# Loading v: two adjacent heads' columns written as one dimension

## The chip, the cores and the metric

The kernel runs on one core of a Trainium2 chip. A core has five engines with their own instruction streams, run in order: PE (matrix multiplication), DVE, ACT and POOL (elementwise work), and SP, which here only issues transfers. Transfers between the chip's main memory and the core's on-chip memory run on 16 DMA engines. The metric is the time of one execution in microseconds, a median of several runs.

## What is computed

An attention without a sequence-squared step, in 8 batches of 8 heads, 576 rows and 64 columns, followed by a mixture of 8 experts with one expert for each row. Cut to what matters:

```python
q_s = softmax(q, axis=-1)          # along the 64 columns
k_s = softmax(k, axis=2)           # along the 576 rows
kv = np.einsum('bhsd,bhse->bhde', k_s, v)
x = np.einsum('bhsd,bhde->bhse', q_s, kv)   # -> 4608 rows of 512
e = argmax(x @ w_gate); g = softmax(x @ w_gate)[e]
out = g * (relu(x @ w1[e]) @ w2[e])
```

## The kernel before

The first 228 us hold the attention, batch by batch, with part of the first expert's work put in between; the rest is a loop over the experts' blocks of rows.

For each batch, the 128 partitions hold two heads of a pair times 64 groups of 9 rows; a tile such as `kt` is 128 partitions x 4 pairs x 9 slots x 64 columns. `kt`, `qt` and `vt` have two buffers each (`KB, VB, QB = 2, 2, 2`), so batch b uses buffer b % 2. `vt` has another layout than the others: slot 0 has 64 columns and a column of ones; the other 8 slots stand in 4 groups of `VW` = 130 columns: a one, slot 1 + 2p, slot 2 + 2p, a one. The product of k and v thus gives the sums of exp(k) too. The two slots of a group are side by side in `vt` (128 columns), and in v itself, where the 9 rows of a group follow each other.

The work is cut into steps, named as in the table `ORDER`, "name.batch.piece". The steps that matter here:

- LK loads k (four pieces for batch 0, one of 1152 KB otherwise), LQ loads q (1152 KB), LV loads v in five pieces: pieces 0 to 3 are one group of two slots each (256 KB, L228), piece 4 is slot 0 (128 KB, L231). All are issued by SP.
- KM0 to KM4 find the maximum of k along the rows (DVE, PE), KS subtracts it (DVE), KE takes exp (ACT, in place in `kt`).
- KV, five pieces, multiplies exp(k) and v on PE (L430): 144 matmuls of 64 columns by 65 for a batch; it goes through slot 0 first, then slot after slot, with 16 matmuls for a slot.
- N0 to N2, G0 to G3 divide by the sums and bring the result to the form that the next product needs (DVE, ACT, PE); QM, QE, QS treat q (DVE, ACT, POOL); TR, EX and MM transpose q and multiply it with kv (L533, L537, L547).
- WG, WH and WL load a piece of the first expert's weights (256 KB, L707) and split it in two parts (L711 on ACT, L715 on POOL); IL loads rows of x sorted by expert (L736); L1 and L4 are that expert's two products (`ph` L758, `py` L773).
- A number at the end of a word in `ORDER`, as in KV.0.0.19, is a number of filler matmuls (L214) put on PE before the step.

`ORDER` fixes the order of all instructions on every engine. Waits are not written out: for each instruction the framework finds which earlier ones wrote or read the same places of a tile, and adds a wait for them. Each transfer gets one of eight semaphores in turn (DMAHW0 to DMAHW7 in the rows below), so a transfer also waits until the one eight transfers before it has landed, where that is not known yet. SP issues in order: what stands behind a waiting transfer waits too.

The lines of the load:

```python
def lv(p):
    if p < FULL:
        nc.sync.dma_start(VT[b % VB][:, :, D + 2 + p * VW:D + 2 + p * VW + 2 * D].rearrange("q c (a d) -> q c a d", a=2),
                          rows_of(v, b)[:, :, 1 + 2 * p:3 + 2 * p])
    else:
        nc.sync.dma_start(VT[b % VB][:, :, :D], rows_of(v, b)[:, :, 0])
```

Of the kernel before, what the change touches and what calls it, by code (L numbers as in the profile page):

```python
# [19 lines left out]
KB, VB, QB = 2, 2, 2  # L20
# [87 lines left out]
class Plan:  # L108
# [3 lines left out]
    def add(self, name, b, i, eng, fn, after=(), take=None, until=(), part=1.0):  # L112
        self.steps[name, b, i] = SimpleNamespace(key=(name, b, i), eng=eng, fn=fn, after=list(after), take=take, until=list(until), part=part)
# [21 lines left out]
def attention_moe(ctx: ExitStack, tc: tile.TileContext, q, k, v, w_gate, w1, w2, xs, out):  # L135
    nc = tc.nc
    B, H, S, D = q.shape
# [6 lines left out]
    J = S // HALF  # L144
# [53 lines left out]
    def rows_of(src, b):  # L198
        return src[b].rearrange("(c i) (p j) d -> (i p) c j d", i=2, j=J)
# [16 lines left out]
    def load(b):  # L216
        o = st[b]
        i = b % 2
        o.kt, o.qt = KT[b % KB], QT[b % QB]
        cut = 1 if b else 4  # L220

        def lk(p):
            cs = slice(p * NP // cut, (p + 1) * NP // cut)
            nc.sync.dma_start(o.kt[:, cs], rows_of(k, b)[:, cs])

        def lv(p):
            if p < FULL:
                nc.sync.dma_start(VT[b % VB][:, :, D + 2 + p * VW:D + 2 + p * VW + 2 * D].rearrange("q c (a d) -> q c a d", a=2),  # L228
                                  rows_of(v, b)[:, :, 1 + 2 * p:3 + 2 * p])
            else:  # L230
                nc.sync.dma_start(VT[b % VB][:, :, :D], rows_of(v, b)[:, :, 0])  # L231

        def lq():
            nc.sync.dma_start(o.qt, rows_of(q, b))

        for p in range(cut):
            add("LK", b, p, SP, lambda p=p: lk(p), rng("KV", b - KB, NV) + [("LK", b, p - 1)], part=1 / cut)
        for p in range(FULL + 1):
            add("LV", b, p, SP, lambda p=p: lv(p), rng("KV", b - VB, NV) + [("LV", b, p - 1)] + ([] if b else rng("LK", 0, 4)), part=2 / 9 if p < FULL else 1 / 9)
        if b == 1:  # L240
            plan.steps["LK", 1, 0].after += rng("LK", 0, 4)
        add("LQ", b, 0, SP, lq, (rng("LK", 0, 4) if b == 0 else []) + rng("QS", b - QB, FULL - 1) + [("QE", b - QB, NP - 1), ("QSR", b - QB, 0)])
# [11 lines left out]
    VW = 2 * D + 2  # L254
    VT = [ka_pool.tile([P, NP, D + 1 + FULL * VW], F32, name=f"vt{i}", bufs=1) for i in range(VB)]
# [1257 lines left out]
```

## Time and profile before

| | |
|---|---|
| time, median of 3 runs | 606.16 us (604.67 to 608.66) |
| profiled execution | 604.79 us, of which the span of the profile is 603.0 us |
| PE busy | 555.1 us (92%) |
| DVE, ACT, POOL busy | 306.3, 232.2, 145.6 us |
| DMA | 87.32 MB, mean 145 GB/s |
| the 32 loads of v of 256 KB, issue to landing | 5.3 us (median) |

PE's busy time holds the filler matmuls, which do no work of the result. Times in the profile are microseconds from the start of the span. In a row of the order of time, brackets give how long the engine had been idle before it and what ended that. "Granted clock" is the share of the full TensorE clock that was granted in a stretch: 1.00 is 2.4 GHz, 0.50 is 1.2 GHz.

### The profile page before, as it was taken

How to read it: one execution, taken by the hardware profiler on the slowest of the kernel's cores; microseconds unless marked ns; L12 is line 12 of the kernel's file. 1: busy time of each engine (PE TensorE's matmuls, PEld its weight loads, DVE VectorE, ACT ScalarE, POOL GpSimd, SP SyncE). 2: the span in 40 equal slices, each digit the busy share in tenths (PEclk: the TensorE clock that was granted, in tenths of full speed). 3: DMA queues.
4: the chain of work that ended last, by engine and by line, in shares of the span. 5: the costliest groups of instructions: out<-in, count | busy, mean ns of one | idle time of the engine just before them, and what ended most of it. 6: DMA issues, size and time to landing. Idle time of an engine off the chain costs nothing.

```text
span 603.0 us, 14677 instructions
## 1 busy us (share of the span) xinstructions
PE 555.1 (92%) x5229; PEld 477.9 (79%) x5230; DVE 306.3 (51%) x604; ACT 232.2 (39%) x499; POOL 145.6 (24%) x261
## 2 busy tenths in 40 slices
PE   8495978899889978999999999999999999999995
PEld 4354657787668757989999898889999898989984
DVE  4365784786865840435505041515652672467354
ACT  1182662564436511234412121314442552364254
POOL 3070743676116461002110101010101101010101
PEclk9777897999899998999999999999999999999999
DMA  5749959768762172369350402030634147045200
GB/s 192 237 117 290 304 146 321 257 205 255 232 209 94 72 296 94 72 235 292 104 140 0 105 0 71 20 89 6 209 123 115 39 170 224 12 143 179 83 17 22
DMA packets 67777, 87.32 MB, mean 145 GB/s; under 512 B 12431, under 2 KB 44175, under 8 KB 67088
## 3 DMA queue, kind: packets, MB, share of 16 engines
q1 hardware_dynamic: 61824, 67.62, 37.0%
q0 software_dynamic: 5904, 19.03, 8.5%
q8 instruction: 34, 0.56, 0.4%
q14 instruction: 15, 0.12, 0.1%
HBM read 63.88 MB, written 23.14 MB: 144 GB/s over the span
## 4 chain that ended last, share of the span: by engine, by line
PE 81%; DMA 9%; issue 3%; DVE 3%; SPq 2%; ACT 1%; DVEq 0%; POOL 0%; POOLq 0%; ACTq 0%
PE py L1072 27%; PE pt L1056 21%; DMA vt<-in_v 7%; PE ph L1056 7%; PE ph L758 6%; PE kv L430 3%; PE py L773 3%; PE xp L547 3%; PE py L1151 2%; PE qT L533 2%; DMA kt<-in_k 1%; PE py L1111 1%; SPq L916 1%; PE mb L387 1%; PE kvT L452 1%
## 5 line engine op out<-in xcount | busy, mean ns | idle before, releaser
L1072 PE MATMUL py<-w2h,hid 128*128 128x512 f32 x480 | 150.1, 390 | 1.8 <-issue 1.8
L1305 DVE SCALAR_TENSOR_TENSOR hid<-pt,hid 128x384 fp32r<-128x384 f32 x72 | 39.5, 556 | 141.7 <-ACT hid L1214 134.4
L1072 PEld LDWEIGHTS py<-w2h,hid 128*128 128x128 f32 x480 | 90.1, 188 | 20.8 <-issue 2.3
L1392 POOL DMA_INDIRECT out<-yt,ix x36 | 38.5, 1069 | 268.9 <-ACT yt L1183 255.5
L1072 PE MATMUL py<-w2l,hid 128*128 128x512 f32 x240 | 93.5, 390 | 0.0
L1183 ACT ACTIVATE yt<-py,ga 128x512 f32<-128x512 f32 x33 | 22.5, 684 | 115.7 <-PE py L1072 93.5
L1214 ACT ACTIVATE hid<-pt 128x384 fp32r<-128x384 f32 x72 | 35.4, 491 | 78.4 <-PE pt L1056 78.4
L1056 PE MATMUL pt<-xh,w1h 128*128 128x384 f32 (+4 forms) x288 | 54.4, 310 | 0.0
L1056 PE MATMUL pt<-xh,w1l 128*128 128x384 f32 (+4 forms) x288 | 54.2, 310 | 0.0
L1056 PE MATMUL pt<-xl,w1h 128*128 128x384 f32 (+4 forms) x288 | 54.2, 310 | 0.0
L1072 PEld LDWEIGHTS py<-w2l,hid 128*128 128x128 f32 x240 | 45.1, 188 | 8.9
L1056 PEld LDWEIGHTS pt<-xh,w1h 128*128 128x128 f32 x288 | 45.9, 189 | 1.2 <-DVE xl L1290 0.3
L1056 PEld LDWEIGHTS pt<-xl,w1h 128*128 128x128 f32 x288 | 45.7, 189 | 0.0
L1056 PEld LDWEIGHTS pt<-xh,w1l 128*128 128x128 f32 x288 | 45.6, 189 | 0.0
L657 POOL DMA_INDIRECT xs<-xr,posi x36 | 35.3, 982 | 26.8 <-DVE own L608 7.6
L430 PE MATMUL kv<-vt,kt 64*64 64x65 f32 x1152 | 26.3, 253 | 15.7 <-DMA vt<-in_v 10.2
L430 PEld LDWEIGHTS kv<-vt,kt 64*64 64x64 f32 x1152 | 24.7, 166 | 16.7 <-issue 14.6
L1284 DVE STREAM_TRANSPOSE xrow<-xt 128x1536 f32<-128x1536 f32 x12 | 35.8, 2981 | 0.7 <-DMA gx<-xs 0.7
L497 POOL TENSOR_TENSOR qs<-qt,qm 128x256 f32<-128x256 f32 x48 | 30.4, 669 | 4.6 <-PE ph L758 4.6
L547 PEld LDWEIGHTS xp<-kx,qTs 64*64 64x64 f32 x1152 | 22.3, 137 | 10.0 <-issue 5.9
L547 PE MATMUL xp<-kx,qTs 64*64 64x73 f32 x1152 | 27.3, 234 | 2.8 <-issue 2.0
L1296 DVE TENSOR_TENSOR w2l<-raw,w2h 128x512 fp32r<-128x512 f32 x40 | 27.2, 686 | 4.9 <-ACT w2h L1207 4.7
(248 smaller groups left out, 913.6 us busy)
## 6 DMA issues: line engine op xcount, KB each, us to landing
raw<-in_moe_w SPq DMA_DIRECT2D x10, 2048.0 KB, 9.0
qt<-in_q SPq DMA_DIRECT2D x8, 1152.0 KB, 8.1
vt<-in_v SPq DMA_DIRECT2D x32, 256.0 KB, 5.3
kt<-in_k SPq DMA_DIRECT2D x7, 1152.0 KB, 7.6
xt<-xs SPq DMA_DIRECT2D x28, 192.0 KB
xt<-xs SPq DMA_DIRECT2D x9, 260.0 KB, 4.7
xs<-zr SPq DMA_DIRECT2D x8, 260.0 KB, 3.3
xt<-in_moe_w SPq DMA_DIRECT2D x8, 256.0 KB, 6.8
```

Source lines behind the costliest of these rows:

```text
L430: nc.tensor.matmul(o.kv[half(m), i, r, lo:lo + D + 1], o.kt[half(i), c, j, :], VT[b % VB][half(i), c, at:at + D + 1], start=False, stop=(j ...
L497: nc.gpsimd.tensor_tensor(to, pairs(o.qt[:, :, j, :]), o.qm[:, :, j].rearrange("p (m r) -> p r m", r=R)[:, :, :, None].to_broadcast([P, R, ...
L547: nc.tensor.matmul(xv[half(a), m, 2 * r + w], o.qT[i][half(m), a * R + r, half(w)], kx[half(m), w, r], start=True, stop=True)
L657: s = nc.gpsimd.indirect_dma_start(out=xs, out_offset=bass.IndirectOffsetOnAxis(ap=n.pi[:, at:at + 1], axis=0), in_=XR[x % 2][:, t, :], in ...
L758: nc.tensor.matmul(I0.ph[f], wt[:, c, f * P:(f + 1) * P], xt[:, c, :], start=(m == 0), stop=(m == len(jobs) - 1))
L1056: m = e.matmul(ph, wt[:, c, f * P:(f + 1) * P], xt[:, c, :w], start=(n == 0), stop=(n == 3 * NC - 1))
L1072: m = e.matmul(g.PY[u], ht[:, f, u * P:(u + 1) * P], wt[:, f, :], start=(n == 0), stop=(n == 3 * NF - 1))
L1214: e.activation(g.HH[:, f, :], g.PH[f][:, :W], AF.Relu).wait_op(sPH[f], it, GE).then_inc(sHH[f], 1)
L1284: e.transpose(g.XR.rearrange("p c (k j) -> p k c j", j=32), xblocks(g.XT).rearrange("p k (l c) -> p k c l", c=NC)).wait_op(sX, ld, GE).the ...
L1296: m = e.tensor_tensor(W2L[:, f, :], g.RAW2[:, f, :], W2H[:, f, :].bitcast(F32), op=ALU.subtract).wait_op(sH2[f], n2, GE)
L1305: e.scalar_tensor_tensor(g.HL[:, f, :], g.PH[f][:, :W], 0.0, g.HH[:, f, :].bitcast(F32), op0=ALU.max, op1=ALU.subtract).wait_op(sHH[f], it ...
L1392: e.indirect_dma_start(out=g.out, out_offset=bass.IndirectOffsetOnAxis(ap=g.IX[:n, u:u + 1], axis=0), in_=g.YT[u][:n], in_offset=None, bou ...
```

## The change

The destination of pieces 0 to 3 is no longer split in two slots of 64 columns; it has three dimensions, the last of 128 columns. The source is the same memory, seen with rows and columns of a partition as one dimension.

```diff
         def lv(p):
             if p < FULL:
-                nc.sync.dma_start(VT[b % VB][:, :, D + 2 + p * VW:D + 2 + p * VW + 2 * D].rearrange("q c (a d) -> q c a d", a=2),
-                                  rows_of(v, b)[:, :, 1 + 2 * p:3 + 2 * p])
+                nc.sync.dma_start(VT[b % VB][:, :, D + 2 + p * VW:D + 2 + p * VW + 2 * D],
+                                  v[b].rearrange("(c i) (p j) d -> (i p) c (j d)", i=2, j=J)[:, :, (1 + 2 * p) * D:(3 + 2 * p) * D])
             else:
                 nc.sync.dma_start(VT[b % VB][:, :, :D], rows_of(v, b)[:, :, 0])
```

No instruction changes its place on any engine. What differs is the waits that the framework adds. SP at the start of the program, the loads of batch 0's v (`vt_95` is buffer 0, `vt_96` buffer 1, `kt_101` and `kt_102` those of k, `qt_103` that of q); "-" before, "+" now:

```order
 L224 DMA kt_102<-in_k 128x4x576
 L228 DMA vt_95<-in_v 128x4x128 [waits Pool_49]
-L228 DMA vt_95<-in_v 128x4x128 [waits DMAHW5_49]
-L228 DMA vt_95<-in_v 128x4x128 [waits DMAHW6_49]
-L228 DMA vt_95<-in_v 128x4x128 [waits DMAHW7_49,DMAHW0_49]
-L231 DMA vt_95<-in_v 128x4x64 [waits DMAHW1_49,DMAHW0_49]
+L228 DMA vt_95<-in_v 128x4x128 x2
+L228 DMA vt_95<-in_v 128x4x128 [waits DMAHW0_49]
+L231 DMA vt_95<-in_v 128x4x64 [waits DMAHW1_49]
 L234 DMA qt_103<-in_q 128x4x576 [waits DMAHW2_49]
```

The first of these loads uses semaphore 5, the next 6, 7, 0 and 1. Before, each has a wait on the semaphore of the load just before it; now the second and third have none, and the last two wait only for the transfer that used their own semaphore before (pieces of k).

The reader of these loads, the first product on PE (KV.0):

```order
 L421 MATMUL kv<-none_115 64x132
 L430 MATMUL kv<-vt_95,kt_101 64x65 [waits DMAHW0_49,DMAHW1_49,Activation_49,Pool_49]
-L430 MATMUL kv<-vt_95,kt_101 64x65 [waits DMAHW5_49,DMAHW6_49,DMAHW2_49,DMAHW7_49,DMAHW0_49,Activation_49]
+L430 MATMUL kv<-vt_95,kt_101 64x65 [waits DMAHW2_49,Activation_49]
 L430 MATMUL kv<-vt_95,kt_101 64x65 x3
 L430 MATMUL kv<-vt_95,kt_101 64x65 [waits DMAHW3_49,Activation_49]
 L430 MATMUL kv<-vt_95,kt_101 64x65 x2
-L430 MATMUL kv<-vt_95,kt_101 64x65 [waits Pool_49]
-L430 MATMUL kv<-vt_95,kt_101 64x65 x63
+L430 MATMUL kv<-vt_95,kt_101 64x65 [waits DMAHW5_49,Pool_49]
+L430 MATMUL kv<-vt_95,kt_101 64x65 x15
+L430 MATMUL kv<-vt_95,kt_101 64x65 [waits DMAHW6_49]
```

The second matmul no longer waits for all pieces; each stretch now waits for its own.

SP after the load of batch 1's q: batch 1's v and the first pieces of batch 2's, then k of batch 2. Before:

```order
L228 DMA vt_96<-in_v 128x4x128 [waits DMAHW3_49]
L228 DMA vt_96<-in_v 128x4x128 [waits DMAHW4_49,DMAHW3_49]
L228 DMA vt_96<-in_v 128x4x128 [waits DMAHW5_49,DMAHW4_49]
L228 DMA vt_96<-in_v 128x4x128 [waits DMAHW6_49,DMAHW5_49]
L228 DMA vt_95<-in_v 128x4x128 [waits DMAHW7_49,PE_49]
L228 DMA vt_95<-in_v 128x4x128 [waits DMAHW7_49,DMAHW0_49]
L231 DMA vt_96<-in_v 128x4x64 [waits DMAHW6_49,DMAHW1_49]
L228 DMA vt_95<-in_v 128x4x128 [waits DMAHW2_49,DMAHW0_49]
L224 DMA kt_101<-in_k 128x4x576 [waits PE_49,Activation_49]
```

Now:

```order
L228 DMA vt_96<-in_v 128x4x128 [waits DMAHW3_49]
L228 DMA vt_96<-in_v 128x4x128 [waits DMAHW4_49]
L228 DMA vt_96<-in_v 128x4x128 [waits DMAHW5_49]
L228 DMA vt_96<-in_v 128x4x128 [waits DMAHW6_49]
L228 DMA vt_95<-in_v 128x4x128 [waits DMAHW7_49,PE_49]
L228 DMA vt_95<-in_v 128x4x128 [waits DMAHW0_49,PE_49]
L231 DMA vt_96<-in_v 128x4x64 [waits DMAHW1_49]
L228 DMA vt_95<-in_v 128x4x128 [waits DMAHW2_49,PE_49]
L224 DMA kt_101<-in_k 128x4x576 [waits DMAHW3_49,PE_49,Activation_49]
```

The waits on the load just before are gone; the loads into `vt_95` each wait for the part of KV.0 that reads their columns, where the first did so for all.

SP with batch 3's v (`vt_96`) and the sorted rows in between (L736). Before:

```order
L228 DMA vt_96<-in_v 128x4x128 [waits DMAHW2_49]
L228 DMA vt_96<-in_v 128x4x128 [waits DMAHW3_49,DMAHW2_49]
L736 DMA xt<-xs 128x520 [waits DMASW3_49,DMASW2_49,DMAHW4_49,DMASW1_49,DMAHW5_49,DMASW0_49,Pool_49]
L736 DMA xt<-xs 128x520
L736 DMA xt<-xs 128x520 [waits DMAHW6_49]
L228 DMA vt_96<-in_v 128x4x128 [waits DMAHW7_49,DMAHW3_49]
L228 DMA vt_96<-in_v 128x4x128 [waits DMAHW7_49,DMAHW0_49]
L231 DMA vt_96<-in_v 128x4x64 [waits DMAHW1_49,DMAHW0_49]
```

Now:

```order
L228 DMA vt_96<-in_v 128x4x128 [waits DMAHW2_49]
L228 DMA vt_96<-in_v 128x4x128 [waits DMAHW3_49]
L736 DMA xt<-xs 128x520 [waits DMASW3_49,DMASW2_49,DMAHW4_49,DMASW1_49,DMAHW5_49,DMASW0_49,Pool_49]
L736 DMA xt<-xs 128x520
L736 DMA xt<-xs 128x520 [waits DMAHW6_49]
L228 DMA vt_96<-in_v 128x4x128 [waits DMAHW7_49]
L228 DMA vt_96<-in_v 128x4x128 [waits DMAHW0_49]
L231 DMA vt_96<-in_v 128x4x64 [waits DMAHW1_49]
```

Here too the second wait of each load of v, on the load before it, is gone, and nothing else.

## Rows read from the trace of the kernel before

**Rows 1.** Chain that ended last, part 4 of the page: shares of the span.

```profile
PE 81%; DMA 9%; issue 3%; DVE 3%; SPq 2%; ACT 1%; DVEq 0%; POOL 0%; POOLq 0%; ACTq 0%
PE py L1072 27%; PE pt L1056 21%; DMA vt<-in_v 7%; PE ph L1056 7%; PE ph L758 6%; PE kv L430 3%; PE py L773 3%; PE xp L547 3%; PE py L1151 2%; PE qT L533 2%; DMA kt<-in_k 1%; PE py L1111 1%; SPq L916 1%; PE mb L387 1%; PE kvT L452 1%
```

**Rows 2.** That chain in order of time, start: start us, us, what.

```profile
3.15 7.98 DMA vt<-in_v
...
11.14 2.82 DMA vt<-in_v
...
19.61 2.35 DMA vt<-in_v
...
26.56 2.42 issue
```

**Rows 3.** Timelines of ACT and PE: start us, us, engine, line, instruction, tiles.

```profile
14.14 2.73 ACT L413 ACTIVATE kt<-kt 128x576 f32<-128x576 f32 x4 [8.08 <-DVE kt L410]
...
22.09 4.47 PE L430 MATMUL kv<-vt,kt 64*64 64x65 f32 x140 [5.42 <-DMA vt<-in_v]
...
46.81 4.11 PE L430 MATMUL kv<-vt,kt 64*64 64x65 f32 x144 [1.67 <-DMA vt<-in_v]
...
88.99 0.25 PE L421 MATMUL kv<-none 64*64 64x132 bf16 x4
92.38 4.41 PE L430 MATMUL kv<-vt,kt 64*64 64x65 f32 x144 [3.14 <-DMA vt<-in_v]
...
123.20 2.29 PE L430 MATMUL kv<-vt,kt 64*64 64x65 f32 x142
```

**Rows 4.** Waits: us in total, times, longest us; SP, then PE to 230 us.

```profile
SPq L228 <- DMA vt<-in_v: 66.5, 19, 8.2
...
SPq L231 <- DMA vt<-in_v: 22.5, 6, 6.6
...
PE kv L430 <- issue: 5.4, 3, 2.8
```

**Rows 5.** The chain in order of time, further: the load of batch 2's k.

```profile
46.80 7.57 DMA kt<-in_k
```

**Rows 6.** Timeline of DVE: after KV.1, before batch 2's maximum, after KV.3.

```profile
50.97 0.17 DVE L437 TENSOR_REDUCE own<-kv 128x4 f32<-128x8 f32 x1 [1.75 <-PE kv L430]
...
54.40 0.69 DVE L364 TENSOR_TENSOR kp<-kt 128x512 f32<-128x512 f32 x1 [2.67 <-DMA kt<-in_k]
...
96.84 0.17 DVE L437 TENSOR_REDUCE own<-kv 128x4 f32<-128x8 f32 x1 [6.00 <-PE kv L430]
```

**Rows 7.** The chain in order of time, further: batch 3's v and what follows.

```profile
71.20 0.35 SPq L228
...
96.79 4.11 PE ph L758 x18
```

**Rows 8.** Stretches: length, busy us of each engine (instructions), granted clock, DMA share, GB/s.

```profile
3.10:11.10 8.00, 8.00 (x41) 4.44 (x40) 2.93 (x5) 1.28 (x1) 3.32 (x29) 1.00 0.82 285
11.10:22.10 11.00, 5.07 (x39) 2.79 (x37) 7.13 (x23) 2.70 (x4) 0.00 (x0) 0.90 0.41 92
22.10:26.50 4.40, 4.40 (x140) 4.22 (x140) 0.00 (x0) 0.00 (x0) 0.00 (x0) 0.50 1.01 378
29.00:71.00 42.00, 34.38 (x724) 24.84 (x724) 27.13 (x64) 21.85 (x63) 21.08 (x30) 0.80 0.73 227
92.40:96.70 4.30, 4.30 (x144) 4.19 (x144) 0.00 (x0) 1.26 (x2) 1.22 (x1) 0.50 0.99 315
123.20:125.40 2.20, 2.20 (x154) 2.20 (x158) 1.33 (x4) 0.60 (x1) 2.04 (x2) 1.00 0.57 217
```

**Rows 9.** DMA packets of the whole run, part 2 of the page.

```profile
DMA packets 67777, 87.32 MB, mean 145 GB/s; under 512 B 12431, under 2 KB 44175, under 8 KB 67088
```

**Rows 10.** The chain in order of time: 18 matmuls of the same kind later on.

```profile
182.06 3.34 PE ph L758 x18
```

**Rows 11.** DMA queues up to 228 us, instruction packets: number, MB, share of 16 engines.

```profile
q8 instruction: 25, 0.41, 0.8%
```

## The prediction

> **What bounds the kernel now.** I began with the chain of work that ended last. It goes by PE for 81% of the span, but 9% of it is transfers, and 7% is the load of v alone [rows 1]. 7% of 603 us is some 42 us, in the attention part, so I read that part of the chain in order of time. It begins with the five loads of batch 0's v [rows 2]: the first lands 8 us after its issue, behind the loads of k; each of the others is issued when the one before it has landed, and takes 2.4 to 2.8 us with nothing beside it. PE starts the first product of k and v (KV.0) at 22.09, after 5.42 us idle for vt [rows 3]. The totals of the waits say the same: SP stood 66.5 us at L228 and 22.5 us at L231 for other loads of v [rows 4]. Since SP issues in order, this also holds back what stands behind: k of batch 2 is issued at 46.80, and DVE waits for it until 54.40 [rows 5, 6]. The third place is KV.3: a row of loads, the first one issued at 71.20, and PE starts at 92.38, after 3.14 us idle [rows 3, 7].
>
> The reader should also see that the DMA engines are not the limit there. From 11.1 to 22.1 us they moved 92 GB/s, from 22.1 to 26.5 us 378 GB/s [rows 8].
>
> **What the change does to the transfers: nothing.** The two slots of 64 columns lie side by side in v and in vt. One could read the edit as runs of 256 bytes made into runs of 512. The page speaks against it: there are 12431 packets under 512 bytes in the whole run [rows 9]; 32 loads of 256 KB in runs of 256 bytes would be 32768 alone. They already went in 512. So this term is nothing. The Trainium skill, "DMA: Bandwidth & Descriptors", section "Specifications", asks for at least 512 B for a transfer at full rate. By that rule and the words of the change, the loads would get faster: by up to the 0.47 us between a lone load of 256 KB and one of 128 KB [rows 2], for seven lone loads in the chain 3 us on top of the sum; by the packet count the rule has nothing to act on, and the count decides.
>
> **What it does to the waits: nearly all.** The order of rows shows it. Before, each load of v waits for the load of the same batch issued before it, although the columns do not overlap; now only the wait for the transfer remains that used the same semaphore eight transfers earlier. Up to eight transfers can be on their way where there was one. On PE, one matmul that waited for all pieces becomes a wait for each group of 16. Priced from below, these cost nothing, being met long before; from above, 40 of them (about five in each of 8 batches) at the 0.13 us that PE took to react to a landing (19.61 + 2.35 to 22.09) are 5.2 us. I take nothing, because the product KV.3 already has a second wait inside and ran its 144 matmuls as one piece [rows 3].
>
> **Term 1, KV.0 starts earlier.** When the first load of v has landed (11.14), 896 KB of batch 0's v remain. Behind the k loads the engines moved 285 GB/s, later 378 [rows 8]: 0.92 MB take 2.4 to 3.2 us, so all is there by 13.5 to 14.3, and by 16.7 with a whole lone load's 2.35 us on top. The other input is exp(k), which ACT ends at 14.14 + 2.73 = 16.87 [rows 3]. PE has work until 22.09 - 5.42 = 16.67 and then stands ready. KV.0 starts near 16.9 in place of 22.09: **5.2 us**.
>
> **Term 2, it runs at the higher clock.** From 22.1 to 26.5 us the granted clock was 0.50, the lower level of 1.2 GHz, after the idle stretch; 140 matmuls took 4.47 us. KV.4, entered from dense work, shows 1.00 (2.4 GHz) and 142 matmuls in 2.29 us [rows 3, 8]. The clock was 1.00 in 3.1 to 11.1 us and PE is busy until 16.67, so I take the fast row: **2.2 us**. The 2.42 us "issue" after it, with an instruction packet on its way, I leave in place: the fetch point moves with KV.0. KV.0 then ends near 22.0, 7.4 us earlier.
>
> **Term 3, KV.1.** PE idled 1.67 us for vt before it [rows 3]. From the start to the end of batch 1's v there are 7680 KB (k and v of two batches and q of two, 1152 KB each, and three weight loads of 256): 21 to 28 us at the two rates, so it lands by about 30, while PE comes to KV.1 at 46.81 - 1.67 - 7.4 = 37.7. KV.1 would gain from the clock as well (4.11 us for 144 matmuls), but DVE, which reads its result, waited only 1.75 us [rows 6] and has work of its own before. So I count **1.75 us**.
>
> **Term 4, k of batch 2.** Its buffer is free when KV.0 is done, now near 22. Ahead of it stand at most q and v of batch 1 and three pieces of v (3072 KB): 8.3 us at 378 GB/s, then its own 7.57 [rows 5]: landed by 38, while DVE comes to it at 54.40 - 2.67 - 1.75 - 7.4 = 42.6. The wait of 2.67 us goes [rows 6]: **2.7 us**. If the load were late all the same, this term would be nothing.
>
> **Term 5, KV.3.** Its loads still stand behind one for KV.4, into the buffer that KV.2 reads: the one issued at 71.20 [rows 7]. From there to 92.38 it was 21 us. Now: 1152 KB of v, 256 of the load ahead, 512 of weights and 780 of sorted rows are 2.76 MB, 7.3 us at 378 GB/s, with some 4 us of issues and 2.4 for the last: 14 at most. PE comes to KV.3 at 88.99 + 0.25, 18 us after that issue, so the 3.14 us go, with 4 us to spare. The clock too: 4.41 us at 0.50 become 2.3 as in KV.4, and the 18 matmuls ph behind it 3.34 for 4.11 [rows 7, 10]. DVE waited 6.00 us for KV.3 [rows 6] and follows: 3.1 + 2.1 + 0.8 = **6.0 us**.
>
> **Term 6, the clock between.** From 29 to 71 us 0.80 was granted [rows 8]. Fewer idle gaps should raise it, but in those stretches DVE, ACT and POOL hand work on too. Bounds: nothing, and 42 x 0.20 = 8.4 us if all of it were PE's time at the full clock. I take **1 us**, near the lower end, since PE's gaps for DVE and POOL remain.
>
> Behind 97 us PE is not seen waiting for v, and in the chain PE follows PE; what is gained earlier is kept, because the other engines follow PE's order. Loads of weights and q that come earlier count nothing: no wait that ends last is theirs.
>
> **Sum.** 5.2 + 2.2 + 1.75 + 2.7 + 6.0 + 1.0 = 18.9 us. The profiled execution took 604.79 us (span 603.0, 1.8 around it): 585.9. The median of the runs shown is 606.16, 1.4 above it; so I forecast **587 us**.
>
> **Rivals.**
> - Only the first wait pays. For it: the loads for KV.3 still stand behind a load that waits for PE, and weights in between wait for POOL. Against it: the 4 us to spare. Terms 1 and 2 and little more: 606 - 8 = 598 us.
> - Nothing moves, 606 us. For it: bytes and packets are the same, and PE is busy for most of the span (fillers included). Against it: DVE stood still 6 us behind KV.3.
> - Slower: PE's own instructions come by DMA, in packets of 16 KB, 25 of them before 228 us [rows 11]. PE stood still for "issue" inside KV three times, 5.4 us in all [rows 4]. With eight loads in flight each fetch could come later. The gain is gone when each of the 25 costs 0.76 us more; at 1.2 us more the kernel takes 587 + 30 = 617 us. Against it: the one within 22 to 29 us, with the engines full, cost 2.42 us, less than the longest, 2.8. The Trainium skill, same page, section "Latency and other measured facts", gives HBM 0.2 us on average and 2 us at high load, which would speak for this rival; these rows do not show it.
> - More than forecast: the clock is full from 12 to 71 us, and the 2.42 us are covered: 587 - 5 = 582 us.
>
> **Chances.** My forecast (583 to 592) 0.65, more gain 0.12, the first wait alone 0.13, nothing 0.05, slower 0.03, and 0.02 for a gain in between. The range of 8 in 10 reaches from 579 to 598. About 1% (6 us) is what a measurement of this kernel can tell from no change: faster 0.92 (all that ends below 600), same 0.05, slower 0.03.
>
> **What would show it.** Right: the loads of batch 0's v issued from 3 us on without landings between, KV.0 starting near 17 with a clock of 1.00, no wait of DVE for k of batch 2, KV.3 following its neighbours without idle time. Wrong on the size: new idle time of PE with "issue" as its end, DVE waiting longer for k or q, weights landing after ACT wants them, or KV.0 still at clock 0.50. Wrong altogether: packets under 512 bytes falling, or KV.0 where it was.

## The result, and the profile after

| | before | after |
|---|---|---|
| time, median of 4 runs | 607.41 us (604.67 to 608.96) | 585.82 us (577.84 to 587.87) |
| profiled execution, span of the profile | 604.79, 603.0 us | 584.83, 583.0 us |
| mean granted clock of the span | 0.967 | 0.982 |

The ratio is 0.9575, with an interval of 0.9456 to 0.9694: 4.25% faster. Ratios and intervals, here and below, leave out runs over 1.5% above the fastest of their kernel, which leaves two of the four of after (584.83 and 577.84 us), and they are not the quotients of the medians, which differ by 3.6% here. Forecast were 587 us and a range of 579 to 598. Between the two profiled executions the span became 20.0 us shorter; the sum of the prediction was 18.9.

Part 2 of the page of after, the line of DMA packets of the whole run:

```profile
DMA packets 67780, 87.37 MB, mean 150 GB/s; under 512 B 12431, under 2 KB 44175, under 8 KB 67088
```

The 12431 packets under 512 bytes are the same as before [rows 9]. The load still moves the same runs; what changed is when it is issued. Part 4, the chain that ended last, in shares of the span:

```profile
PE 86%; DVE 4%; issue 4%; ACT 3%; SPq 2%; POOL 0%; DVEq 0%; POOLq 0%; ACTq 0%
```

Transfers had 9% [rows 1] and are no longer in it at all. "issue", time in which an engine waits for nothing that the profile shows, went from 3% to 4%. The timeline of SP (start us, us, line, transfer, number in a row):

```profile
3.15 4.37 SPq L228 DMA_DIRECT2D vt<-in_v  x4
7.56 2.94 SPq L231 DMA_DIRECT2D vt<-in_v  x1
...
26.46 0.77 SPq L224 DMA_DIRECT2D kt<-in_k  x1
...
57.94 1.59 SPq L228 DMA_DIRECT2D vt<-in_v  x2
68.06 0.98 SPq L228 DMA_DIRECT2D vt<-in_v  x2
69.09 0.52 SPq L231 DMA_DIRECT2D vt<-in_v  x1
```

All five loads of batch 0's v are issued by 10.5 us, none of them waiting for another, and k of batch 2 at 26.46, where it was 46.80 [rows 5]. The median time of a 256 KB load of v from issue to landing rose from 5.3 to 7.2 us, with several now on their way at once. PE does not wait for them: the waits of PE up to 230 us have no row for vt any more. They begin:

```profile
PE kv L430 <- issue: 8.1, 4, 3.8
PE ph L758 <- DVE hid L764: 3.1, 4, 1.1
```

(us in total, times, longest us.) What grew is the first row: 8.1 us for 5.4 [rows 4]. The timeline of PE shows where:

```profile
15.98 2.62 PE L430 MATMUL kv<-vt,kt 64*64 64x65 f32 x140
21.00 0.33 PE L430 MATMUL kv<-vt,kt 64*64 64x65 f32 x4 [2.41 <-issue]
...
36.98 0.86 PE L430 MATMUL kv<-vt,kt 64*64 64x65 f32 x43
38.86 1.74 PE L430 MATMUL kv<-vt,kt 64*64 64x65 f32 x101 [1.03 <-issue]
...
54.72 1.47 PE L430 MATMUL kv<-vt,kt 64*64 64x65 f32 x83
60.01 1.46 PE L430 MATMUL kv<-vt,kt 64*64 64x65 f32 x43 [3.82 <-issue]
...
62.24 0.74 PE L430 MATMUL kv<-vt,kt 64*64 64x65 f32 x14
...
77.75 2.27 PE L430 MATMUL kv<-vt,kt 64*64 64x65 f32 x144
...
105.63 2.30 PE L430 MATMUL kv<-vt,kt 64*64 64x65 f32 x144
```

These are KV.0, KV.1, KV.2, KV.3 and KV.4. KV.0, KV.1 and KV.3 no longer begin after idle time that a load ends, and they run at 16 to 20 ns for each matmul where KV.0 and KV.3 took 31 to 32 [rows 3]. Inside KV.2 there is a pause of 3.82 us that was not there before. It costs more than its length: the granted clock was 1.00 ahead of it (54.70 to 56.20 us) and 0.50 behind it (60.00 to 62.98 us), so that the 83 matmuls ahead took 18 ns each and the 43 behind 34. KV.2 before, from its first row to its last:

```profile
67.97 2.36 PE L430 MATMUL kv<-vt,kt 64*64 64x65 f32 x125
...
70.69 0.44 PE L430 MATMUL kv<-vt,kt 64*64 64x65 f32 x15
```

DVE's timeline, the rows that answer to [rows 6], with the one after KV.2 between:

```profile
41.16 0.15 DVE L437 TENSOR_REDUCE own<-kv 128x4 f32<-128x8 f32 x1
41.81 0.68 DVE L364 TENSOR_TENSOR kp<-kt 128x512 f32<-128x512 f32 x1
63.03 0.17 DVE L437 TENSOR_REDUCE own<-kv 128x4 f32<-128x8 f32 x1 [4.03 <-PE kv L430]
...
80.10 0.17 DVE L437 TENSOR_REDUCE own<-kv 128x4 f32<-128x8 f32 x1 [0.58 <-PE kv L430]
```

DVE no longer waits for KV.1 (1.75 before) or for k of batch 2 (2.67), and 0.58 us for KV.3 in place of 6.00. It waits 4.03 us for KV.2 instead.

### The profile page after: what moved, and what is told of

Its sections match the earlier page's. It is cut to its first block, busy times and chain, and to the rows that moved or that the text cites. A ratio compares the mean times of both kernels' runs of the same rounds, so it can differ in the third digit from the quotient of the medians.

```text
span 583.0 us, 14654 instructions
## 1 busy us (share of the span) xinstructions
PE 546.2 (94%) x5229; PEld 471.0 (81%) x5230; DVE 305.3 (52%) x604; ACT 232.3 (40%) x499; POOL 144.1 (25%) x261
## 2 busy tenths in 40 slices
DMA packets 67780, 87.37 MB, mean 150 GB/s; under 512 B 12431, under 2 KB 44175, under 8 KB 67088
## 4 chain that ended last, share of the span: by engine, by line
PE 86%; DVE 4%; issue 4%; ACT 3%; SPq 2%; POOL 0%; DVEq 0%; POOLq 0%; ACTq 0%
PE py L1072 28%; PE pt L1056 22%; PE ph L1056 7%; PE ph L758 6%; PE xp L547 3%; PE py L773 3%; PE kv L430 3%; PE py L1151 2%; PE qT L533 2%; PE hot L214 2%; PE py L1111 1%; SPq L916 1%; PE mb L387 1%; PE kmT L214 1%; PE pt L741 1%
## 5 line engine op out<-in xcount | busy, mean ns | idle before, releaser
L497 POOL TENSOR_TENSOR qs<-qt,qm 128x256 f32<-128x256 f32 x48 | 29.1, 641 | 4.6 <-PE ph L758 4.6
L430 PE MATMUL kv<-vt,kt 64*64 64x65 f32 x1152 | 21.7, 225 | 8.1 <-issue 8.1
L1290 DVE TENSOR_TENSOR xl<-xrow,xh 128x1536 fp32r<-128x1536 f32 x11 | 19.3, 1759 | 17.1 <-ACT xh L1198 17.1
```

Of the source, the lines that this page charges most:

```text
L430: nc.tensor.matmul(o.kv[half(m), i, r, lo:lo + D + 1], o.kt[half(i), c, j, :], VT[b % VB][half(i), c, at:at + D + 1], start=False, stop=(j ...
L497: nc.gpsimd.tensor_tensor(to, pairs(o.qt[:, :, j, :]), o.qm[:, :, j].rearrange("p (m r) -> p r m", r=R)[:, :, :, None].to_broadcast([P, R, ...
```

## The experiments

Two theories stood against each other, and a third concerns the size. The first: the false waits of one piece of v for another were the cost, in three places (batch 0; batches 1 and 2 with k of batch 2; batch 3). The second: the form of the transfer itself (longer runs, or fewer dimensions) makes it faster. The third: instructions of PE that arrive late take part of the gain. Each kernel has runs of the kernel before beside it: their median is 609.18 us for e1 to e4, 607.69 us for e5 to e8. The last column is read from the one profiled execution of each kernel, which can be some us from its median.

| | median us | ratio to before | "issue" of PE in KV to 230 us |
|---|---|---|---|
| e1_batch0 | 598.82 | 0.9783 [0.9701, 0.9865] | 9.1 us |
| e2_batch12 | 604.33 | 0.9927 [0.9894, 0.9961] | 14.5 us |
| e3_batch3 | 601.04 | 0.9839 [0.9763, 0.9916] | 7.0 us |
| e4_halves | 597.32 | 0.9787 [0.9722, 0.9851] | 18.3 us |
| e5_four_dims | 585.50 | 0.9628 [0.9580, 0.9676] | 9.6 us |
| e6_k3_earlier | 581.26 | 0.9562 [0.9512, 0.9613] | 9.0 us |
| e7_batches0to3 | 590.01 | 0.9670 [0.9611, 0.9728] | 9.8 us |
| e8_no_fillers | 592.51 | 0.9732 [0.9683, 0.9782] | 14.0 us |

### One part of the change at a time

e1_batch0, e2_batch12 and e3_batch3 use the new form for some batches and the old one for the rest. Of e1:

```diff
-            if p < FULL:
+            if p < FULL and (b == 0):
+                nc.sync.dma_start(VT[b % VB][:, :, D + 2 + p * VW:D + 2 + p * VW + 2 * D],
+                                  v[b].rearrange("(c i) (p j) d -> (i p) c (j d)", i=2, j=J)[:, :, (1 + 2 * p) * D:(3 + 2 * p) * D])
+            elif p < FULL:
```

Behind it stands the load in its old form. e2 has `(b in (1, 2))` there, e3 `(b == 3)`.

> Only batch 0's v is loaded in the new form; batches 1 to 7 keep the old form with its waits. Theory (the waits between loads of v are the cause, and each place pays for itself): KV.0 starts at 16 to 17 us in place of 22.09 and ends 8 us earlier; DVE still waits for k of batch 2, and PE still stands idle for vt before KV.3; all later places move by about 8 us: 598 us (596 to 600). Rival (the first places are the whole cause, later waits vanish by themselves once the start is earlier): 586 to 590 us. Rival (the form of the load does not matter here): 606 us.

Measured: 598.82 us, as expected, a ratio of 0.9783, and a span of 598.3 us. PE's timeline, KV.0, KV.1, KV.3 and KV.5:

```profile
16.39 2.62 PE L433 MATMUL kv<-vt,kt 64*64 64x65 f32 x140
...
39.80 4.16 PE L433 MATMUL kv<-vt,kt 64*64 64x65 f32 x144 [4.97 <-DMA vt<-in_v]
...
83.61 3.85 PE L433 MATMUL kv<-vt,kt 64*64 64x65 f32 x144 [2.48 <-DMA vt<-in_v]
...
141.32 3.27 PE L433 MATMUL kv<-vt,kt 64*64 64x65 f32 x141 [2.21 <-DMA vt<-in_v]
```

(The edit moves line 430 to 433.) KV.0 does what it does in after. What is late next is KV.1's v: PE waits 4.97 us for it, where it was 1.67 [rows 3], since PE comes earlier and the loads do not. DVE still waits 0.53 us for k of batch 2.

> Only batches 1 and 2 are loaded in the new form. Theory: KV.0 stays at 22 us; k of batch 2 is issued well before 46.8 us and DVE no longer waits for it (2.67 us), PE's 1.67 us before KV.1 go; KV.3 still waits for vt: 4 to 6 us less, 600 to 602 us. Rival (only the start counts): 606 us.

Measured: 604.33 us, 0.9927, a small gain, and less than the 4 to 6 us expected (600 to 602 us). The waits went where expected: KV.0 still waits (4.95 us), DVE does not wait for k of batch 2, KV.3 waits 3.02 us. But KV.2 has a pause of its own:

```profile
63.76 1.47 PE L433 MATMUL kv<-vt,kt 64*64 64x65 f32 x83
71.24 1.46 PE L433 MATMUL kv<-vt,kt 64*64 64x65 f32 x43 [6.02 <-issue]
```

6.02 us that the kernel before did not have. The gain between the medians is 4.85 us; the trace is of the slowest of its ten runs (609.02 us), so how much of the pause is in that gain is not known.

> Only batch 3 is loaded in the new form. Theory: nothing moves before 71 us; the 3.14 us idle before KV.3 go, KV.3 runs in 2.3 us at granted clock 1.00 in place of 4.41 us at 0.50, and DVE follows: 6 us less, 600 us (598 to 602). If what PE loses to late instructions inside KV.2 in the changed kernel (3.82 us) comes from the loads of batch 3 that are then on their way, it shows here too. Rival (the slack is absorbed elsewhere): 606 us.

Measured: 601.04 us, within the 598 to 602 expected, 0.9839. KV.3 starts at 87.65 without idle time and takes 2.27 us, and KV.2 shows no pause. The next load in line is that of KV.5:

```profile
87.65 2.27 PE L433 MATMUL kv<-vt,kt 64*64 64x65 f32 x144
...
145.47 3.77 PE L433 MATMUL kv<-vt,kt 64*64 64x65 f32 x141 [5.17 <-DMA vt<-in_v]
```

So each part pays by itself (e2 by less than 1%, with an interval that stays below 1), and after each of e1 and e3 it is the next load that still waits falsely that is late. The pause in KV.2 comes when batches 1 and 2 load early or KV.0 is early (e1: 3.06 us), not from batch 3's loads.

### The waits without the longer runs

e4_halves drops the false waits in the other direction: each piece becomes two loads of one slot, of 64 columns.

```diff
-                nc.sync.dma_start(VT[b % VB][:, :, D + 2 + p * VW:D + 2 + p * VW + 2 * D].rearrange("q c (a d) -> q c a d", a=2),
-                                  rows_of(v, b)[:, :, 1 + 2 * p:3 + 2 * p])
+                for h in range(2):
+                    at = D + 2 + p * VW + h * D
+                    nc.sync.dma_start(VT[b % VB][:, :, at:at + D], rows_of(v, b)[:, :, 1 + 2 * p + h])
```

> Every load of two slots is split into two loads of one slot, 128 KB each, in runs of 256 bytes, with no wait between them. Twice the transfers, half the run length, none of the false waits. Theory (waits): nearly all of the gain stays, 586 to 594 us, less what 32 more issues of 0.37 us on SP and half the bytes on their way per semaphore cost; packets under 512 bytes rise by 32768 to some 45200. Rival (run length is the cause): 606 us or more.

Measured: 597.32 us, 0.9787: expected were 586 to 594, so this missed. The line of packets of its page, and KV.0, KV.2 and KV.3 in PE's timeline:

```profile
DMA packets 84673, 87.32 MB, mean 146 GB/s; under 512 B 45711, under 2 KB 61071, under 8 KB 83984
```

```profile
16.20 2.61 PE L431 MATMUL kv<-vt,kt 64*64 64x65 f32 x141
22.57 0.48 PE L431 MATMUL kv<-vt,kt 64*64 64x65 f32 x3 [3.76 <-issue]
...
64.93 1.46 PE L431 MATMUL kv<-vt,kt 64*64 64x65 f32 x43 [5.96 <-issue]
...
88.59 2.23 PE L431 MATMUL kv<-vt,kt 64*64 64x65 f32 x72 [3.95 <-issue]
```

Here the runs really are of 256 bytes, with 33280 more packets under 512. KV.0 starts at 16.20 all the same, 5.9 us before its old place, and no matmul waits for vt. The short runs were slower on their way: from 11 to 13 us, where loads of v are most of the traffic, the engines are full in e4 (first row) and in after (second row; columns as in [rows 8]), and move 211 and 295 GB/s.

```profile
11.00:13.00 2.00, 1.49 (x13) 0.82 (x14) 1.45 (x13) 0.00 (x0) 0.00 (x0) 1.00 1.13 211
11.00:13.00 2.00, 1.48 (x14) 0.73 (x13) 1.68 (x14) 0.00 (x0) 0.00 (x0) 1.00 1.21 295
```

But no reader waited for them. What was lost is mostly in "issue": 18.3 us in KV for 8.1 in after. These 10.2 us are most of the 15.5 between the two profiled executions (600.28 and 584.83 us; between the medians it is 11.5). Whether the slower runs had a part in that, by keeping the engines full for longer, was not tested; between before and after the runs are the same, so it does not touch their difference.

e5_four_dims goes back to four dimensions, with the same memory and the same waits as after: the destination and the source are both split by `rearrange("q c (a d) -> q c a d", a=4)`, four runs of 32 columns, where before had `a=2` and two runs of 64.

> The destination is again written with four dimensions, but as four runs of 32 columns in place of two of 64. The waits are those of the changed kernel. Theory (the waits are the cause, not the number of dimensions): the time of the changed kernel, 586 us (578 to 590). Rival (a destination of four dimensions is slow in itself): 606 us, and other packet counts.

Measured: 585.50 us, 0.9628, with the same span as after, 583.0 us; KV.0 starts at 16.22. Its page counts the same 12431 packets under 512 bytes as before and after, and SP waits for no other load of v. So the number of dimensions costs nothing by itself, and the gain belongs to the waits. Whether the framework drops them for the new source or for the new destination is not known, since e5 changes both against before.

### The pause in KV.2

e6_k3_earlier is after with one step moved: the load of batch 3's k (LK.3.0) stood in `ORDER` behind KV.2.2 and EV.1.3 and now follows LQ.2.0. The aim was that it should not be on its way while KV.2 runs.

```diff
-KM2.2.0 G3.1.0 KM3.2.0 MM.1.0.1 WG.0.6 MM.1.1 LQ.2.0 DE.1.0 EX.1.2 ...
+KM2.2.0 G3.1.0 KM3.2.0 MM.1.0.1 WG.0.6 MM.1.1 LQ.2.0 LK.3.0 DE.1.0 EX.1.2 ...
-EV.1.2 WH.0.6 KV.2.0 ... KV.2.2 EV.1.3 LK.3.0 EX.1.4 ...
+EV.1.2 WH.0.6 KV.2.0 ... KV.2.2 EV.1.3 EX.1.4 ...
```

> The changed kernel, with batch 3's k issued right after batch 2's q, ahead of a weight load that waits for POOL (LK.3.0 moved ahead of WG.0.7 in the order). It then lands before KV.2 begins, in place of being on its way during it. Theory A (the 3.82 us without instructions inside KV.2 come from data that is queued ahead of PE's instruction packet): the stall falls to under 2.5 us, KV.2 ends 1.5 to 4 us earlier, 582 to 585 us. Theory B (the stall comes from where the packet border falls, whatever is on its way): the stall stays at 3.5 to 4 us and the time at 586 us.

Measured: 581.26 us, 0.9562, the lowest median of this study. But the pause is still there, at the same matmul. SP and the load's time to landing, then PE:

```profile
44.26 0.46 SPq L224 DMA_DIRECT2D kt<-in_k  x1
...
kt<-in_k SPq DMA_DIRECT2D x1, 1152.0 KB, 11.5
```

```profile
53.01 1.44 PE L430 MATMUL kv<-vt,kt 64*64 64x65 f32 x83
58.09 1.46 PE L430 MATMUL kv<-vt,kt 64*64 64x65 f32 x43 [3.65 <-issue]
```

3.65 us for 3.82, after the 83rd matmul as in after. By the expectation this would speak for theory B, but the move did not do what it was for. The load was issued 9.8 us earlier (54.06 us in after) and took 11.5 us to land, 8.0 in after: it landed at about 55.8 us, when PE had already stood for 1.3 us. So data was on its way all the same, and the run does not decide between A and B. Nor is the gain of some 4 us over after explained by the move: KV.1 already starts at 34.78 for 36.98, and up to there the two programs have the same order. KV.2, KV.3, KV.4 and KV.5 are each 1.5 to 1.7 us earlier than in after, and the rest of the span gives 1.4 more. The intervals of e5 and e6 overlap. Whether the move helps is open.

e8_no_fillers takes the 19 filler matmuls away that stand ahead of KV.0 (KV.0.0.19 becomes KV.0.0). It asks whether KV.0 owes its fast clock to what PE does before it, and it moves every later instruction of PE forward by 38 (19 matmuls with their weight loads).

> The changed kernel without the 19 filler matmuls ahead of KV.0. PE then stands idle for 3.2 us before it, though nothing else is late. Theory (term 2: what PE did just before sets the clock of KV.0): the granted clock of KV.0 is 0.50 and it takes 4 to 4.5 us, 2 us more than with fillers, 587 to 589 us. Rival (the idle stretch has to be longer than 3 us): the clock stays 1.00, KV.0 2.3 to 2.6 us, 586 us.

Measured: 592.51 us, 0.9732, some 7 us more than after; 587 to 589 were expected, so the time missed. PE's timeline at KV.0, and the stretches ahead of it and over it (the columns are those of [rows 8]):

```profile
15.82 0.30 PE L430 MATMUL kv<-vt,kt 64*64 64x65 f32 x2 [2.15 <-ACT kt L413]
16.44 0.35 PE L430 MATMUL kv<-vt,kt 64*64 64x65 f32 x8 [0.32 <-ACT kt L413]
17.10 3.65 PE L430 MATMUL kv<-vt,kt 64*64 64x65 f32 x134 [0.32 <-ACT kt L413]
```

```profile
12.50:16.00 3.50, 1.34 (x16) 0.72 (x15) 3.40 (x16) 1.65 (x3) 0.00 (x0) 1.00 1.10 357
16.00:20.00 4.00, 3.36 (x117) 3.11 (x119) 3.17 (x6) 1.05 (x2) 0.00 (x0) 0.61 0.98 289
```

PE was busy for only 1.34 of the 3.5 us ahead, and KV.0 then ran at a granted clock of 0.61, near the lower level of 1.2 GHz: 27 ns for a matmul where it was 19. Yet this is not where the 7 us are: KV.0 ends at about 20.75, earlier than in after (21.33), because its pause of 2.41 us is gone with the moved instructions. The others grew:

```profile
38.27 1.49 PE L430 MATMUL kv<-vt,kt 64*64 64x65 f32 x82 [2.90 <-issue]
...
59.71 1.03 PE L430 MATMUL kv<-vt,kt 64*64 64x65 f32 x26 [5.23 <-issue]
...
84.68 1.44 PE L430 MATMUL kv<-vt,kt 64*64 64x65 f32 x54 [3.82 <-issue]
```

In all 14.0 us for 8.1: 5.9 of the 10.2 us between the two profiled executions (595.02 and 584.83 us; 6.7 between the medians), with 38 instructions fewer ahead of them.

PE's instructions come in packets of 16 KB over the same DMA engines [rows 11]. That these packets are PE's is read from two things: from the first to the fourteenth of them in before, PE went through 1581 weight loads and as many matmuls, 243 for each packet; and each pause of PE in KV ended 1.2 to 1.6 us after one of them. Counted from the records of that queue, the packet on which the pause in KV.2 ended or would have ended (the sixth of the run):

```
kernel          weight loads of PE done by then   packet starts   takes   PE stopped for
before          728                               66.50 us        1.09    no pause in KV.2
e3_batch3       732                               66.63 us        1.07    no pause in KV.2
after           852                               57.64 us        0.94    3.82 us
e6_k3_earlier   852                               55.77 us        0.96    3.65 us
e8_no_fillers   852                               57.35 us        0.93    5.23 us
e4_halves       853                               62.50 us        0.95    5.96 us
```

In the first two the packet begins some 120 matmuls before PE has used up what it has; in the others only when PE has stopped already: 1.3 and 1.45 us after the end of the row ahead of the pause in e6 and after (53.01 + 1.44 and 54.72 + 1.47), 2.9 and 3.5 us in e8 and e4. It takes no longer there, and PE goes on some 1.4 us after its end. So in these rows the pause is made by a packet that starts late, not by one that takes long. (In e1, with 3.06 us in KV.2, the packet starts when PE stops and takes 1.73.)

Why it starts late was not tested, but the traces lean one way. Two stretches of after, up to PE's stop and from there to the packet's start, and the second of these in e6 (the last column but one is the DMA engines' share; about 1 is full):

```profile
52.40:56.20 3.80, 3.38 (x128) 2.72 (x127) 3.20 (x10) 3.80 (x9) 3.12 (x4) 1.00 0.42 112
56.19:57.64 1.45, 0.00 (x0) 0.00 (x0) 1.45 (x2) 0.19 (x1) 1.45 (x2) 1.00 0.87 231
54.45:55.77 1.32, 0.00 (x0) 0.00 (x0) 1.32 (x2) 0.02 (x1) 0.87 (x1) 1.00 1.05 413
```

The DMA engines had room before PE stopped in after (0.42), but hardly any while it stood and the packet had not begun (0.87), and none in e6 (1.05), in e8 (1.01 from 54.48 to 57.35 us) and in e4 (0.97 from 58.98 to 62.50 us). The third packet of the run shows the other side: in e1, with idle engines in the microsecond before it (0.00), it starts when PE has done 347 weight loads; in after and e6, with full ones (1.11 and 1.04), after 393 and 471. This speaks for a packet that waits behind data, which is theory A of e6 and a rival of the prediction. It is not shown: no run empties the engines under KV.2, and in before the sixth packet comes in time with the engines as full (1.05 from 65.50 to 66.50 us), beside slower work of PE.

### Only the first four batches

e7_batches0to3 uses the new form for `b < 4` (the diff of e1 with that condition). It asks whether the last four batches gain as well.

> Batches 0 to 3 in the new form, 4 to 7 in the old. The prediction counted nothing for the later batches, since PE did not wait for their v before the change. Theory (as predicted): 586 us. Rival (once everything is earlier, batch 5's row of waiting loads is what is late next, as the 2.2 to 5.2 us of PE before KV.5 in the kernels with one part changed suggest): PE waits 3 to 6 us for vt before KV.5, and the time is 588 to 592 us.

Measured: 590.01 us, 0.9670. SP does wait falsely again, 30.5 us in all for other loads of v (L231 is the old form's line here):

```profile
SPq L231 <- DMA vt<-in_v: 30.5, 6, 10.2
```

But no matmul waits for vt, at KV.5 neither: there the expectation missed. Of the 5.6 us between its span and that of after (588.6 and 583.0 us), the first part is not made by those waits: its KV.2 begins at 57.57, 2.85 us later than in after, and ahead of it stand 2.9 us of "issue" at a filler; KV.3, KV.4 and KV.5 are all 2.6 or 2.7 late. The second part may be: KV.7 begins 5.7 us late (173.38 for 167.69). The pause in KV.6 is 2.36 us for 0.80, and behind it PE ran at a granted clock of 0.56 (158.50 to 162.35 us), in after at 1.00 (154.37 to 156.66 us). In before and e1 to e3, whose last four batches load in the old form too, that pause is 2.8 to 3.9 us; in after, e5 and e6 it is 0.8 to 1.8. So the late waits may cost through PE's instructions without a wait of PE for v. It was not shown: e8 and e4, which have no false waits either, have 2.0 and 2.7 us there, and the intervals of e5 and e7 overlap.

## Why the prediction was right, step by step

**The transfers.** "Nothing" was right: the same packets, and neither 256-byte runs (e4) nor a fourth dimension (e5) made a reader of v wait. The words of the change suggest longer runs; the count of packets said that there were none. (The two slots that it joins are neighbouring rows of one head, 64 numbers each, not columns of two heads as the title has it.) The Trainium skill, "DMA: Bandwidth & Descriptors", section "Specifications", wants at least 512 B for full rate. Between before and after it had nothing to act on. In e4 it had, and the trace agrees with it, with 211 GB/s for 295 on full engines; but no reader waited for the shorter runs.

**Terms 1 and 2.** KV.0 was to start near 16.9 and end 7.4 us earlier. It started at 15.98, 6.1 earlier, and its last four matmuls ended at 21.33 for 29.31: 8.0 us. The 140 matmuls took 2.62 us (2.3 forecast), and the 2.42 us of "issue" stayed, as 2.41. e8 agrees that the clock hangs on what PE does ahead of KV.0: with the fillers gone it was 0.61, where it was 1.00.

**Terms 3 and 4.** DVE was to come to batch 2's maximum 11.85 us earlier (7.4 + 1.75 + 2.7): it came at 41.81 for 54.40, 12.6 us earlier, with both waits gone.

**Term 6.** 1 us forecast; between there and the start of KV.2 the lead grew from 12.6 to 13.25 us. The granted clock from 29 to 71 us (the same times, so partly other work) rose from 0.80 to 0.92:

```profile
29.00:71.00 42.00, 33.97 (x804) 25.81 (x803) 27.45 (x70) 23.67 (x70) 21.57 (x30) 0.92 0.74 245
```

Taken at the upper bound this would have been 5 us (42 x 0.12). It brought little; the value near the lower end was right.

**Term 5 and what the sum left out.** KV.3 lost its wait (3.1 us) and ran in 2.27 us for 4.41, as forecast. But KV.2 between them was not in the sum: it begins 13.25 us earlier and ends only 8.15 earlier, at 62.98 for 71.13. This is part of the third rival (late packets of instructions), which was priced as a mean over 25 packets; what came was one pause of 3.82 us in one place, and the lower clock behind it. From there to the end of KV.3 the lead grows again by 8.6 us, to 16.8, where term 5 alone forecast 3.1 + 2.1 = 5.2: the other engines went on during the pause and PE had less to wait for (between KV.2 and KV.3 it was idle for 1.2 us of 14.7, before for 3.8 of 17.9). With the 18 matmuls ph behind KV.3 (3.36 us for 4.11) the lead is 17.5 us, for 18.9 forecast.

**Behind 97 us.** "What is gained earlier is kept" held: 17.6 us at KV.4, 17.5 at KV.5. Then two pauses shrank, of 2.05 and 2.76 us before, of 1.50 and 0.80 after, which the prediction did not have:

```profile
134.53 0.49 PE L547 MATMUL xp<-kx,qTs 64*64 64x73 f32 x17 [1.50 <-issue]
...
153.57 0.68 PE L430 MATMUL kv<-vt,kt 64*64 64x65 f32 x28 [0.80 <-issue]
```

With the stretches around them the lead is 21.4 us where the attention ends (206.68 for 228.09 at L1158), and 20.0 at the end; why the experts' loop gave back 1.4 us is open. So the total agrees to 1.1 us by luck, because two errors nearly cancel: some 5 us lost in KV.2, and some 6 us that PE made up behind it and in the later pauses. "PE is not seen waiting for v behind 97 us" held for after and e7. It fails where only an early part is changed: in e1, e2 and e3 KV.5 waits 2.2, 2.2 and 5.2 us.

**The rivals.** Only the first wait pays: e1 is that kernel, at 598.82 us for the 598 worked out, but the other places pay too. Nothing moves: out. Late instructions: the mechanism is real, and the pauses are 10 us longer in e4 and nearly 6 in e8 than in after, but they never took all of the gain. More gain (582 us, the pauses covered): the pauses stayed, though one execution of after took 577.84.

## What to carry to other kernels

Before a transfer is blamed for its size, see in the order of waits whether pieces of one tile wait for each other: a queue that stands for other loads of the same tile while the engines move a quarter of what they move right after (92 and 378 GB/s) may be held by a wait that the framework added, and another way to write the same destination may remove it (here 20 of 603 us). Do it for all pieces of the chain, since with one part mended the next false wait is late. And look again for "issue" inside PE's densest stretch of small matmuls: it moved by up to 10 us with small changes of the program, enough to hide half of a gain.

## What was not expected of the hardware

Instructions that arrive late stop PE for up to 6.0 us at a time, mostly inside KV, where PE goes through 144 matmuls and as many weight loads in 2.3 us. The packet itself takes about 1 us (0.9 to 2.2), and PE goes on 1.2 to 1.6 us after it. The place of the pause follows the count of instructions (behind the 83rd matmul of KV.2 in after, e2, e5, e6 and e7; behind the 101st in e8, which has 19 matmuls fewer ahead of it), its length does not. And behind the pause the clock can be the lower one: 0.50 to the end of KV.2 in after.

Loads in runs of 256 bytes moved 211 GB/s on full engines (e4), loads in runs of 512 some 295 (after), and yet KV.0 started at 16.20 and 15.98 us. And after PE was busy for 1.34 of 3.5 us, the granted clock over the next 4 us was 0.61 (e8), with 1.00 in the stretch before.
